# One fused attention and MLP kernel: another order of the prologue's steps, dummy products spread over it, and new tables behind it

## The chip, the cores and the metric

The kernel runs on one core of a Trainium2 chip. The metric is the device time of one execution in microseconds (us), as the median of several runs; less is better. Five engines work side by side, each through its own list of instructions in order: TensorE (PE, matrix products; its weight loads are shown as PEld), VectorE (DVE), ScalarE (ACT), GpSimd (POOL), and SyncE (SP), whose list issues nearly all transfers. An instruction starts when those before it on its engine have begun or ended and the semaphores that it waits for are there.

## What is computed

The reference, cut to what matters (8 batches, 8 heads, 576 tokens, head size 64; 4608 tokens of width 512, a hidden width of 2048):

```python
q_c, k_c, v_c = (a.reshape(B, H, nc, 64, D) for a in (q, k, v))
scores = np.matmul(q_c, k_c.transpose(0, 1, 2, 4, 3)) / np.sqrt(D)
attn = np.exp(scores - np.max(scores, axis=-1, keepdims=True))
attn = attn / (np.sum(attn, axis=-1, keepdims=True) + 1e-09)
x = np.matmul(attn, v_c).reshape(B, H, S, D).transpose(0, 2, 1, 3).reshape(B * S, H * D)
r = np.maximum(x @ w_in, 0.0)
out = (s * (r * r) + b) @ w_out
```

Each chunk of 64 tokens attends to itself alone; then every token goes through a squared-ReLU layer.

## The kernel before

**Numbers as pairs.** A float32 operand is split into a high part (names ending in h: `xh`, `wh`, `gh`) that TensorE takes in one pass and the remainder (`xl`, `wl`, `gl`). Each product is three: high by high, high by low, low by high.

**The prologue** (class `First`) does the first four token blocks of 128 with plain products while the weights are unpacked. There are 16 weight pairs, each a tile of 128 x 1024 in two halves .0 and .1, and pairs of w_in and w_out alternate: up 0 and 1 use pair 0, up 2 and 3 pair 1, down 0 and 1 pair 2, and so on. A pair goes through these steps: `load` (SP, into one of three `raw` buffers), `scale` and `tail` (ScalarE, L214 and L218), `shift` and `sign` (VectorE, L224 and L226), `add` (POOL, L232; it frees the raw buffer), `hi` (ScalarE, L236, makes `wh`), `lo` (VectorE, L240, makes `wl`), and `keep` (SP, L248, writes them to memory as `kept`). TensorE uses a pair in `up` and `more` (L904, x by w_in) or in `down` (L929, g by w_out); `left` is the first half of the columns of up 0. After an `up`, `relu` and `copy` (ScalarE, L909 and L913) and `rest` (VectorE, L917) make g and free its PSUM bank, of which there are two.

**Attention** of two token blocks takes the steps `load_qk`, `load_v`, `scores` (TensorE, L320), `peak` (VectorE, L325), `sub` (VectorE, L329), `exp` (ScalarE, L334), `sum` (VectorE, L338), `invert` (VectorE, L345 and L346), `scale` (L349: POOL for pair a, VectorE for pair b), `transposes` (TensorE, L356), `copies` (ScalarE, L361), `values` (TensorE, L383), `x_hi` (ScalarE, L406) and `x_lo` (VectorE, L410). Pairs .a and .b are the prologue's own; numbers (scores.0 and on) are the following block's, and a name like `2:scores.0` belongs to the block after that. From the fourth block on `turn` (VectorE, L367) and `swap` (SP, L376, eight small transfers) take the place of `transposes` and `copies`.

**Dummy products.** `keep_busy` (L179) multiplies a tile of ones by itself into a bank that nobody reads: steps `busy0` to `busy5` with 8, 6, 12, 2, 4 and 2 products. `scalars` (TensorE, L960) and `scalars_out` (VectorE, L963) bring the two scalars s and b into place.

**Behind the prologue** four blocks of eight token blocks use products of a Strassen-like kind (`1:p0` to `1:p57` in block 1; L839, L574, L623, 12 products each). The weights come back from `kept` through six buffers: `1:st6` is the transfer (L547) of the seventh. `combine`, `combined_hi`, `combined_lo` and `keep_combined` (L266, L272, L276, L279) form sums of weight quarters and write them to `kept` for these products, beside the products of block 1. `x_sums` (L505) forms sums of x.

**What sets the order.** Every step is a function under a name. The string `ORDER` lists 781 names, from the first load to the end of block 1, and the last line of the kernel calls them in that order, so the order of each engine's and each queue's instructions is that of the string. The blocks behind it follow a planner's rule. The string `SLOTS` gives each new SBUF tile its home: the number of one of 45 places of 4 KB per partition, in the order in which tiles are made. A tile that takes a place waits for those who still use what was there. The scheduler adds no order of its own (`tc.manual_schedule()`).

```python
order = ORDER.split()
for previous, block in zip([None] + blocks, blocks):
    order += [name for name in block.order(previous) if name not in order]
for name in order + blocks[-1].pre[-1]:
    ops[name]()
```

Of the kernel before, what the change touches and what calls it, by code (L numbers as in the profile page):

```python
# [31 lines left out]
scores.0 sign3.0 add2 relu0 rest1 peak.0 up3 copy0 rest0 lo1 load5 hi2 up2 tail3 lo2 keep2 more2 scale4 add3.0 sub.0
down0 load_v.0 tail4 shift4 hi3.0 sign4 relu2 down1 lo3.0 exp.0 add4 copy2 sum.0 scale5 rest2 tail5 more3 norm.0
add3.1 load6 up4 hi4 load7 hi3.1 more4 relu3 keep1 lo4 transposes.0 2:load_v.1 copies.0 shift5 down2 lo3.1 copy3 relu4
sign5 scale6 rest3 add5 up5 copy4 shift6 tail6 more5 load8 sign6 load_v.1 values.0 relu5 rest4 add6 scale7 down3 copy5
hi5 rest5 shift7 load9 hi6 up6 sign7 keep0 x_hi.0 lo5 x_out.0 up7 lo6 tail7 more6 scale8 x_lo.0 add7 more7 relu6
shift8 scores.1 tail8 load10 down4 relu7 sign8 scale9 peak.1 add8 copy7 down5 copy6 rest7 hi7 rest6 shift9 load11 hi8
lo7 keep3 tail9 up9 lo8 tail10 sign9 up8 scale10 sub.1 add9 more9 shift10 more8 relu9 down6 load12 copy9 sign10 keep7
exp.1 keep6 relu8 add10 sum.1 down7 load_v.2 copy8 rest9 hi9 norm.1 load13 tail11 up10 scale11 rest8 hi10 shift11
transposes.1 lo9 keep9 copies.1 up11 lo10 tail12 sign11 scale12 more10 more11 relu10 shift12 add11 sign12 values.1  # L40
down8 x_hi.1 load15 relu11 2:load_v.0 x_lo.1 add12 copy11 down9 hi11 keep8 rest11 copy10 x_out.1 rest10 load14 lo11
scale13 scores.2 keep5 hi12 shift13 up13 peak.2 tail13 keep4 sub.2 up12 load_qk.3 lo12 exp.2 more13 scale15 sum.2
more12 tail15 load_v.3 norm.2 down10 relu13 sign13 relu12 keep11 shift15 transposes.2 scale14 add13 down11 copy12
copy13 keep12 copies.2 rest13 shift14 hi13 values.2 rest12 tail14 sign14 up15 x_hi.2 lo13 add14 x_lo.2 up14 sign15
x_out.2 more14 hi14 more15 lo14 add15 scores.3 relu15 relu14 down12 peak.3 copy15 sub.3 stream hi15 down13 copy14 lo15
exp.3 rest14 rest15 2:load_qk.0 down14 sum.3 keep14 norm.3 last 1:combine0.7 keep13 transposes.3 copies.3 1:combine0.6
down15 values.3 1:combine1.0 steady 1:p0 x_hi.3 out0 x_lo.3 out1 1:p2 1:combine1.1 1:combined_hi0.7 x_out.3
1:keep_combined0.7.0 keep10 1:combine0.5 1:p1 keep15 1:combine1.2 1:combined_hi0.5 1:p4 1:combined_hi0.6
1:keep_combined0.5.0 1:combined_hi1.0 1:combine0.4 1:relu11.0 2:scores.0 1:combined_lo0.5 1:combined_hi0.4 1:p5
2:peak.0 1:combined_hi1.2 1:keep_combined0.4.0 1:combined_lo0.6 1:keep_combined1.2.0 1:combined_lo0.4 1:p6  # L50
1:keep_combined0.6.1 1:relu12.0 1:st6 1:st7 2:sub.0 2:load_qk.1 1:combined_hi1.1 1:combined_lo1.0 1:p3 2:exp.0
1:combined_lo0.7 1:combined_lo1.1 1:p7 1:relu21.0 2:sum.0 1:keep_combined1.1.1 2:norm.0 1:p8 2:turn.0 1:x_sums.0
2:swap.0.7 2:swap.0.4 1:p9 1:keep_combined0.6.0 2:swap.0.1 1:keep_combined0.5.1 1:x_sums.1 2:swap.0.3 1:p10 2:swap.0.0
1:xh2.1 2:swap.0.6 1:relu22.0 2:swap.0.5 1:combine1.3 1:keep_combined0.4.1 1:keep_combined0.7.1 1:p12 2:swap.0.2
1:xh3.1 1:xh4.0 1:keep_combined1.1.0 1:combine1.4 1:xh4.1 1:relu11.1 1:p11 1:st10 1:st11 1:combine1.5 1:xh2.0 1:gh0.0
1:p13 1:relu21.1 1:combined_lo1.2 1:st9 1:keep_combined1.0.1 1:combine1.6 2:values.0 1:st8 1:p14 2:x_out.0 1:xl4.0
1:combined_hi1.3 1:combined_hi1.4 1:keep_combined1.3.0 1:combined_lo1.3 1:keep_combined1.0.0 2:scores.1 1:xh3.0
1:xl2.1 1:xh6.0 1:relu12.1 1:xl2.0 1:p15 1:xl6.0 2:peak.1 1:st13 2:sub.1 1:p16 1:st12 2:load_qk.2 1:xl3.0 2:exp.1
1:xl3.1 1:keep_combined1.2.1 1:relu22.1 1:xl4.1 1:p17 2:sum.1 1:st15 1:keep_combined1.4.0 1:combined_lo1.4 1:keep0.2
1:xh6.1 2:norm.1 1:p18 1:combined_hi1.6 1:xl6.1 2:turn.1 1:p19 1:keep2.2 1:gl0.0 2:swap.1.4 2:swap.1.2 1:keep3.2  # L60
1:combine1.7 2:swap.1.6 1:st22 1:p21 2:swap.1.1 2:swap.1.7 1:form11.2 2:swap.1.3 1:st16 1:combined_lo1.6 1:st14
1:square11.2 1:p23 1:st18 1:keep_combined1.3.1 1:form21.2 1:p20 1:st17 1:keep0.3 2:swap.1.5 1:gh0.1 2:swap.1.0
1:keep_combined1.4.1 1:square21.2 1:p24 1:form22.2 1:less11.0 1:combined_hi1.5 1:gl0.1 1:p22 1:square22.2
1:keep_combined1.5.0 1:st19 1:less11.1 1:st20 1:keep3.3 2:values.1 1:st23 1:gh0.2 1:p25 2:x_out.1 1:gl0.2 1:form12.2
1:combined_lo1.5 1:less12.1 1:keep_combined1.5.1 2:scores.2 2:load_qk.3 1:keep2.3 1:less12.0 1:gh3.1 1:p26 1:st24
1:keep_combined1.6.1 2:peak.2 2:sub.2 1:p27 1:st28 1:form11.3 1:less11.2 1:square11.3 1:p28 1:gl3.1 1:st21 1:gh4.1
1:t2.0 1:combined_hi1.7 1:t2.1 1:p30 2:exp.2 1:keep_combined1.7.0 1:form21.3 1:st25 1:gh1.1 1:form22.3 1:p31 1:st26
1:combined_lo1.7 1:square22.3 2:sum.2 1:gh3.0 1:p32 2:norm.2 1:st27 1:keep_combined1.6.0 1:gh4.2 1:keep_combined1.7.1
1:less12.2 1:gh0.3 1:p29 1:gh1.0 column_sums 1:gl3.0 1:gh3.2 2:turn.2 1:p34 1:form12.3 1:gl0.3 2:swap.2.1 2:swap.2.7
1:combine0.2 1:st31 1:st29 2:xh0.0 1:p33 2:swap.2.5 1:gh2.0 1:less11.3 2:swap.2.6 1:gh1.2 2:swap.2.3 1:gl1.1  # L70
2:swap.2.2 1:square21.3 1:st30 1:gl3.2 1:st38 2:swap.2.4 1:less12.3 biases 1:p35 1:gh4.0 1:gh3.3 1:gl4.1 1:p36 1:st34
1:gh2.1 2:load_v.2 1:gl3.3 1:keep0.down 2:swap.2.0 1:gl2.0 1:p37 1:st32 1:t2.2 1:t2.3 1:gh2.2 1:gl1.2 1:p38 1:gh2.3
1:st33 1:keep3.down 1:gl2.1 1:gl1.0 2:values.2 1:st47 1:gl2.2 1:p39 2:x_out.2 1:gl2.3 2:xh0.1 1:combine0.0 1:gh5.0
finish 2:scores.3 1:st35 2:load_v.3 1:gl4.0 1:p40 2:peak.3 1:gh5.3 2:sub.3 1:p42 1:st36 1:less21.0 2:exp.3 1:gh5.2
2:sum.3 1:combined_hi0.0 1:less21.1 1:p41 1:st39 1:combined_hi0.2 1:combine0.1 2:xh1.0 1:gh1.3 1:p43 2:xl1.0 1:st41
1:combined_hi0.1 2:norm.3 1:gh6.0 1:keep2.down 2:turn.3 1:p44 1:gh6.1 1:combined_lo0.0 2:swap.3.3 1:gh4.3 1:st40
1:gh5.1 1:p46 1:gl4.2 1:st42 1:keep_combined0.0.1 2:xh1.1 2:swap.3.5 1:gl4.3 2:swap.3.0 1:combined_lo0.2 1:p47 1:st37
1:gl5.3 1:gl6.0 1:p48 1:st43 1:gl1.3 2:swap.3.2 1:keep_combined0.2.0 1:gl5.0 1:keep_combined0.1.0 1:p49 1:st46
1:less21.3 2:swap.3.7 2:swap.3.1 1:less21.2 2:swap.3.6 1:combine0.3 2:swap.3.4 1:gh6.2 1:p45 1:keep_combined0.0.0
1:gh6.3 1:st44 1:gl6.2 2:xh5.0 1:combined_hi0.3 1:p50 1:gl6.3 1:st45 1:gl6.1 1:combined_lo0.1 1:p51 2:xl5.0  # L80
1:keep_combined0.1.1 1:st49 1:gl5.2 1:gl5.1 2:values.3 1:st48 3:load_qk.0 1:end11 1:p52 2:x_out.3 3:load_v.0 1:end00
2:x_sums.1 2:xl0.1 1:p54 2:st1 store 1:p53 2:st0 2:x_sums.0 2:xh6.1 2:xh5.1 2:xl6.1 1:p55 2:st4 2:xh4.0 2:xh3.1
1:end10 1:scaled00 2:xl0.0 1:p56 1:scaled10 2:xl3.1 2:xh2.1 1:store10 2:xh3.0 1:store00 1:p57 2:xh2.0 2:st2 2:xl3.0
2:st3 2:xh6.0 1:keep_combined0.3.0 2:xh4.1 2:xl4.0 1:end01 2:xl2.0 2:xl6.0 1:scaled11 2:xl1.1 2:xl5.1 2:xl2.1
1:store11 2:xl4.1 1:combined_lo0.3 1:keep_combined0.3.1 1:keep_combined0.2.1 2:st5
"""


# [992 lines left out]
```

## Time and profile before

| | |
|---|---|
| time, median of 3 runs | 786.87 us (786.78 to 787.15) |
| the profiled execution | 787.23 us; span from its first to its last instruction 785.4 us |
| TensorE busy | 770.5 us (98%) |
| VectorE, ScalarE, POOL busy | 547.6, 486.1, 156.5 us |
| mean granted clock of TensorE | 0.993 of full speed |
| transfers | 206.42 MB, 263 GB/s on average |

The profile shows one execution. Spans of instructions are in us from the first instruction; "idle before <-" names what ended the time in which the engine stood still. A matmul of float32 operands is shown as two rows, so 14 dummy products are 28 rows. Matmuls overlap, so the spacing of their starts is their cost, not the length of one. The span and the 1.83 us around it make up the execution's own time.

### The profile page before, as it was taken

Reading aid. Unit: us, or ns where it says so; the run is one execution under the profiler, and the core shown is the slowest. Engines: PE = TensorE matmul, PEld = TensorE weight load, DVE = VectorE, ACT = ScalarE, POOL = GpSimd, SP = SyncE. Lnnn points to the kernel's source line nnn. Section 1 sums busy time; section 2 is a strip of 40 time slices with the busy share of each in tenths; the row PEclk is TensorE's granted clock in tenths of the full one; section 3 lists DMA queues with packets and bytes.
Section 4 is the critical chain, followed back from the end, with each engine's and each line's share of the span. In section 5 each row is a group of like instructions: output and inputs, shape, how many; then the busy total and the mean of one; then the engine's idle time right before and its main releaser. Section 6 shows DMA issues by size and latency. Waiting matters only on the chain.

```text
span 785.4 us, 13747 instructions
## 1 busy us (share of the span) xinstructions
PE 770.5 (98%) x5538; PEld 634.6 (81%) x5538; DVE 547.6 (70%) x569; ACT 486.1 (62%) x582; POOL 156.5 (20%) x74
## 2 busy tenths in 40 slices
...
GB/s 321 283 274 331 332 383 300 294 281 368 348 306 267 224 374 360 264 291 246 214 255 168 280 256 279 291 172 285 187 270 225 239 251 193 189 192 195 200 217 108
DMA packets 86818, 206.42 MB, mean 263 GB/s; under 512 B 8036, under 2 KB 37988, under 8 KB 86756
## 3 DMA queue, kind: packets, MB, share of 16 engines
...
q10 hardware_dynamic: 148, 0.13, 0.1%
...
## 4 chain that ended last, share of the span: by engine, by line
PE 94%; DVE 2%; ACT 2%; issue 1%; DMA 1%; DVEq 0%; SPq 0%; ACTq 0%
PE ps_o L623 26%; PE ps_o L574 25%; PE ps L623 11%; PE ps L574 10%; PE ps_h L904 4%; PE ps_o L929 4%; PE ps_o L839 4%; PE ps L839 2%; PE ps_a L383 2%; PE ps_a L317 2%; PE ps_o L638 1%; PE ps_h L179 1%; DVE wl L240 1%; PE ps_a L356 1%; DMA qk<-in_qkv_dram 1%
## 5 line engine op out<-in xcount | busy, mean ns | idle before, releaser
L623 PE MATMUL ps_o<-gh,st 128*128 128x512 f32 x608 | 190.7, 390 | 0.0
L602 DVE TENSOR_TENSOR gl<-q,gh 128x1024 fp32r<-128x1024 f32 x112 | 156.4, 1425 | 47.6 <-ACT gh L597 45.5
L574 PE MATMUL ps_o<-xh,st 128*128 128x512 f32 x560 | 180.9, 392 | 0.0
L623 PEld LDWEIGHTS ps_o<-gh,st 128*128 128x128 f32 x608 | 114.1, 188 | 24.0
L597 ACT CAST gh<-q 128x1024 fp32r<-128x1024 f32 x112 | 113.4, 1047 | 28.5 <-DVE q L610 28.2
L610 POOL TENSOR_TENSOR q<-q 128x1024 f32<-128x1024 f32 x24 | 66.6, 2782 | 323.3 <-PE ps_o L574 212.6
L574 PEld LDWEIGHTS ps_o<-xh,st 128*128 128x128 f32 x560 | 105.1, 188 | 23.6 <-DMA st<-kept 0.3
L623 PE MATMUL ps_o<-gl,st 128*128 128x512 f32 x304 | 118.3, 389 | 0.0
L574 PE MATMUL ps_o<-xl,st 128*128 128x512 f32 x280 | 109.1, 390 | 0.0
L455 DVE TENSOR_TENSOR q<-ps_o,tmp 128x1024 f32<-128x1024 f32 x28 | 34.3, 1224 | 77.7 <-PE ps_o L574 59.8
L623 PE MATMUL ps<-gh,st 128*128 128x512 f32 x256 | 81.4, 391 | 0.0
L574 PE MATMUL ps<-xh,st 128*128 128x512 f32 x224 | 73.5, 389 | 0.0
L580 ACT ACTIVATE q<-q 128x1024 f32<-128x1024 f32 x42 | 44.3, 1054 | 36.4 <-DVE q L455 36.4
L623 PEld LDWEIGHTS ps_o<-gl,st 128*128 128x128 f32 x304 | 57.1, 188 | 11.7
L574 PEld LDWEIGHTS ps_o<-xl,st 128*128 128x128 f32 x280 | 52.6, 188 | 10.3
L449 ACT COPY tmp<-ps_o 128x1024 f32<-128x1024 f32 x37 | 37.3, 1008 | 37.5 <-PE ps_o L574 22.7
L610 DVE TENSOR_TENSOR q<-q 128x1024 f32<-128x1024 f32 x40 | 50.4, 1269 | 13.0 <-ACT q L593 12.6
L505 POOL TENSOR_TENSOR xt<-xf 128x512 f32<-128x512 f32 x12 | 21.8, 1814 | 185.4 <-DMA st<-kept 168.3
L880 ACT ACTIVATE o<-o,bias,sb 128x512 f32<-128x512 f32 x28 | 21.1, 807 | 57.8 <-DVE o L455 57.8
L232 POOL TENSOR_TENSOR f<-f,raw 128x1024 int32<-128x1024 int32 (+1 forms) x18 | 41.8, 2322 | 73.9 <-DVE f L226 30.0
L623 PEld LDWEIGHTS ps<-gh,st 128*128 128x128 f32 x256 | 48.0, 188 | 10.1
L623 PE MATMUL ps<-gl,st 128*128 128x512 f32 x128 | 49.8, 389 | 0.0
...
## 6 DMA issues: line engine op xcount, KB each, us to landing
st<-kept SPq DMA_DIRECT2D x218, 512.0 KB, 4.4
qk<-in_qkv_dram SPq DMA_DIRECT2D x36, 512.0 KB, 5.9
raw<-in_w_dram SPq DMA_DIRECT2D x32, 512.0 KB, 7.0
kept<-wh SPq DMA_DIRECT2D x20, 512.0 KB, 5.9
...
out_dram<-o SPq DMA_DIRECT2D x17, 512.0 KB, 6.5
kept<-f SPq DMA_DIRECT2D x16, 512.0 KB, 6.3
...
```

What stands on the lines that cost most here:

```text
L232: nc.gpsimd.tensor_tensor(out=i, in0=i, in1=low.bitcast(I32), op=ALU.add)
L449: nc.scalar.copy(out=self.u[product], in_=self.bank_of(product))
L455: nc.vector.tensor_tensor(out=to, in0=self.ps[bank], in1=self.u[kept], op=ALU.add)
L574: nc.tensor.matmul(out=to[:, k], lhsT=a[:, cols], rhs=x[:, c, :], start=i in BEGINS and c == 0 and n == 0, stop=c == 1 and n == 2, skip_gr ...
L580: nc.scalar.activation(out=q, in_=q, func=AF.Relu)
L597: nc.scalar.copy(out=self.g[i, pp][0], in_=self.q[quarter, pp])
L602: nc.vector.tensor_tensor(out=lo, in0=self.q[quarter, pp], in1=hi.bitcast(F32), op=ALU.subtract)
L610: engine.tensor_tensor(out=self.q[to, pp], in0=self.q[x, pp], in1=self.q[y, pp], op=ALU.subtract)
L623: nc.tensor.matmul(out=self.to[i][:, d], lhsT=a[:, cols], rhs=x[:, k, :], start=i in BEGINS and pp == 0 and k == 0 and n == 0, stop=pp == ...
L839: nc.tensor.matmul(out=bank[:, k], lhsT=a, rhs=x[:, c, :], start=d == 0 and c == 0 and n == 0, stop=d == 1 and c == 1 and n == 2)
L904: nc.tensor.matmul(out=self.h[j][:, cols], lhsT=w[c][low], rhs=x[:, c, :], start=low + c + i == 0, stop=low == 1 and c == NHP - 1)
L929: nc.tensor.matmul(out=self.acc[d], lhsT=a, rhs=x, start=(j == 0 and i == 0), stop=(j == NJ - 1 and i == 2))
```

## The change

Two strings are replaced: `ORDER`, with the same 781 names in another order, and `SLOTS`. Nothing else differs: the number of dummies in each `busy` step, the functions and the planner stay. The first lines of `ORDER` and one line of each table:

```diff
@@ -24,85 +24,85 @@
 ORDER = """
-load_qk.a load0.0 load_qk.b load0.1 load_v.a scores.a load1 busy0 peak.a load2 tail0.0 busy1 scale0.0 sub.a scalars
-busy2 shift0.0 exp.a scalars_out sign0.0 busy3 load_v.b busy4 sum.a add0.0 scores.b invert.a hi0.0 peak.b scale.a
...
+load_qk.a busy0 load0.0 load_qk.b load0.1 load_v.a scores.a load1 scalars peak.a busy1 load3 tail0.0 scale0.0 sub.a
+scores.b shift0.0 exp.a sign0.0 load_v.b add0.0 sum.a busy2 tail0.1 scalars_out invert.a hi0.0 peak.b scale.a scale0.1
...
 SLOTS = """
...
-43 44 1 2 3 4 7 5 11 10 8 18 0 14 15 25 27 24 28 30 34 21 26 31 39 40 22 9 23 13 42 1 32 33 25 15 27 28 21 3 10 13 43
...
+43 44 1 2 3 4 7 5 11 10 0 8 16 14 15 22 21 31 32 25 41 20 23 33 37 38 24 42 29 44 9 18 15 22 11 16 20 13 29 30 34 31
...
```

What this does to the instructions is read at three places. In such a list a dummy row counts products, not the profile's rows.

TensorE at the start of the program, before the change. `qk` feeds scores.a and, in its second row, scores.b; `ident,p` are transposes.a and .b, `pT,v` values.a and .b, `ones` the dummies, `sb_row` the scalars, and `xh,wh` the first product of the layer:

```order
L320 MATMUL ps_o<-qk 64x64 x32
L179 MATMUL ps_h<-ones 128x128 x14
L960 MATMUL ps_h<-ident,sb_row 128x1 x2
L179 MATMUL ps_h<-ones 128x128 x18
L320 MATMUL ps_o<-qk 64x64 x32
L356 MATMUL ps_a<-ident,p 128x128 x8
L383 MATMUL ps_o<-pT,v 64x64 x32
L356 MATMUL ps_a<-ident,p 128x128 x8
L383 MATMUL ps_o<-pT,v 64x64 x32
L179 MATMUL ps_h<-ones 128x128 x2
L904 MATMUL ps_h<-xh,wh 128x256
```

The same place after the change:

```order
L179 MATMUL ps_h<-ones 128x128 x8
L320 MATMUL ps_o<-qk 64x64 x32
L960 MATMUL ps_h<-ident,sb_row 128x1 x2
L179 MATMUL ps_h<-ones 128x128 x6
L320 MATMUL ps_o<-qk 64x64 x32
L179 MATMUL ps_h<-ones 128x128 x12
L356 MATMUL ps_a<-ident,p 128x128 x8
L179 MATMUL ps_h<-ones 128x128 x2
L383 MATMUL ps_o<-pT,v 64x64 x32
L179 MATMUL ps_h<-ones 128x128 x4
L356 MATMUL ps_a<-ident,p 128x128 x8
L179 MATMUL ps_h<-ones 128x128 x2
```

Of the 32 dummies that stood between scores.a and scores.b six are left there; eight stand ahead of scores.a, and the others between the later attention steps.

VectorE in the same stretch, as a difference: from sub.a and shift0.0 (`f<-f`) by sign0.0 (`f<-raw,f`), sum.a (`z<-p`) and the copy of the scalars (`sb<-ps_h`) to invert.a (`z<-z`):

```order
 L329 TENSOR_TENSOR p<-ps_o,m 128x2x8x64
 L224 TENSOR_SCALAR f<-f 128x512
+L226 SCALAR_TENSOR_TENSOR f<-raw,f 128x512
+L338 TENSOR_REDUCE z<-p 128x16
 L963 COPY sb<-ps_h 128x2
-L226 SCALAR_TENSOR_TENSOR f<-raw,f 128x512
-L338 TENSOR_REDUCE z<-p 128x16
 L345 TENSOR_SCALAR z<-z 128x16
 L346 RECIPROCAL z<-z 128x16
```

The copy of the scalars has moved behind sign0.0 and sum.a.

SP beside the first streamed products of block 1, before the change: `kept<-wh` and `kept<-f` are keep_combined, `st<-kept_1_81 x2` are st6 and st7, `qk` the next block's load, `pT<-pB` swaps:

```order
L279 DMA kept_2_82<-wh 128x4x256 x2
L279 DMA kept_1_85<-wh 128x4x256
L279 DMA kept_3_83<-f 128x4x256
L547 DMA st<-kept_1_81 128x1024 x2
L294 DMA qk<-in_qkv_dram 128x1024 x2
L279 DMA kept_0_84<-f 128x4x256
L376 DMA pT<-pB 32x512 x2
```

The same place after the change:

```order
L294 DMA qk<-in_qkv_dram 128x1024 x2
L302 DMA v<-in_qkv_dram 128x512 x2
L279 DMA kept_3_83<-wh 128x4x256
L547 DMA st<-kept_1_81 128x1024
L376 DMA pT<-pB 32x512
L547 DMA st<-kept_1_81 128x1024
L376 DMA pT<-pB 32x512 x4
```

A swap, which waits for `turn`, now stands between st6 and st7.

## Rows read from the trace of the kernel before

**Rows 1.** The page, part 1: busy time and its share of the span.

```profile
PE 770.5 (98%) x5538; PEld 634.6 (81%) x5538; DVE 547.6 (70%) x569; ACT 486.1 (62%) x582; POOL 156.5 (20%) x74
```

**Rows 2.** What TensorE waited for: us in total, times, longest us.

```profile
PE ps_o L320 <- DMA qk<-in_qkv_dram: 4.3, 1, 4.3
PE ps_o L383 <- ACT pT L361: 3.8, 2, 3.1
PE ps_a L356 <- DVE p L349: 1.9, 1, 1.9
PE ps_o L929 <- DVE wl L240: 0.9, 1, 0.9
```

**Rows 3.** The chain of waits, 0 to 40 us: start us, us, what.

```profile
5.63 1.13 PE ps_o L320 x32
6.76 4.32 PE ps_h L179 x28
11.28 4.21 PE ps_h L179 x36
15.50 1.14 PE ps_o L320 x64
17.91 1.23 DVE p L329
22.51 1.22 DVE p L349
37.86 2.40 PE ps_h L904 x9
```

**Rows 4.** Stretches, `ps_h` alone: us, PE, PEld, DVE, ACT, clock, DMA share, GB/s.

```profile
8.00:8.50 0.50, 0.50 (x4) 0.50 (x4) 0.00 (x0) 0.00 (x0) 1.00 1.07 442
9.50:10.00 0.50, 0.50 (x7) 0.50 (x6) 0.00 (x0) 0.00 (x0) 1.00 0.95 377
```

**Rows 5.** Stretch, all work: us, PE, PEld, DVE, ACT, POOL, clock, DMA, GB/s.

```profile
23.00:32.65 9.65, 8.11 (x90) 7.52 (x91) 8.85 (x11) 7.51 (x12) 2.40 (x1) 0.50 0.96 352
```

**Rows 6.** Timeline of VectorE: start us, us, instruction [idle before].

```profile
11.32 0.16 DVE L963 COPY sb<-ps_h 128x2 f32<-128x2 f32 x1 [1.68 <-PE ps_h L960]
21.96 0.63 DVE L240 TENSOR_TENSOR wl<-f,wh 128x512 fp32r<-128x512 f32 x1
27.47 2.29 DVE L240 TENSOR_TENSOR wl<-f,wh 128x512 fp32r<-128x512 f32 x1 [0.80 <-ACT wh L236]
29.69 1.27 DVE L410 TENSOR_TENSOR xl<-ps_o,xh 128x512 fp32r<-128x512 f32 x2
```

**Rows 7.** Timeline of POOL.

```profile
14.00 1.90 POOL L349 TENSOR_TENSOR p<-p,z 128x1024 f32<-128x1024 f32 x1 [0.46 <-DVE z L346]
26.81 2.40 POOL L232 TENSOR_TENSOR f<-f,raw 128x1024 int32<-128x1024 int32 x1 [5.18 <-DVE f L226]
34.03 2.75 POOL L232 TENSOR_TENSOR f<-f,raw 128x1024 int32<-128x1024 int32 x1 [4.82 <-DVE f L226]
```

**Rows 8.** Transfers issued between 2.55 and 3.06: KB, us to landing.

```profile
qk<-in_qkv_dram SPq DMA_DIRECT2D x1, 512.0 KB, 7.0
```

**Rows 9.** Timeline of ScalarE.

```profile
28.54 0.59 ACT L406 CAST xh<-ps_o 128x512 fp32r<-128x512 f32 x1 [0.27 <-PE ps_o L383]
```

**Rows 10.** Stretches, all work, columns as in rows 5.

```profile
31.00:121.00 90.00, 89.00 (x817) 72.88 (x816) 78.92 (x89) 78.53 (x116) 36.77 (x15) 0.99 0.93 320
121.00:291.00 170.00, 170.00 (x1280) 139.35 (x1281) 154.60 (x202) 109.26 (x128) 2.78 (x2) 1.00 0.91 311
```

**Rows 11.** The chain of waits, 150 to 170 us.

```profile
156.98 8.16 PE ps_o L839 x36
```

**Rows 12.** Block 1: SP and VectorE timelines; transfers issued 119 to 300 us.

```profile
148.96 2.36 SPq L547 DMA_DIRECT2D st<-kept  x2
156.88 1.25 DVE L367 STREAM_TRANSPOSE pB<-p 128x1024 f32<-128x1024 f32 x1
st<-kept SPq DMA_DIRECT2D x53, 512.0 KB, 5.8
```

More of the change, by code (lines that the diff above doesn't have):

```diff
@@ L26 @@
 ORDER = """
-load_qk.a load0.0 load_qk.b load0.1 load_v.a scores.a load1 busy0 peak.a load2 tail0.0 busy1 scale0.0 sub.a scalars
-busy2 shift0.0 exp.a scalars_out sign0.0 busy3 load_v.b busy4 sum.a add0.0 scores.b invert.a hi0.0 peak.b scale.a
-scale0.1 tail0.1 sub.b shift0.1 exp.b transposes.a sign0.1 copies.a sum.b add0.1 values.a scale1 invert.b load3 tail1
-lo0.0 load_qk.0 scale.b x_hi.a load_qk.2 shift1 transposes.b x_lo.a copies.b values.b sign1 hi0.1 x_hi.b busy5 lo0.1
-add1 left x_lo.b scale3 up1 scale2 shift3 tail2 load4 more1 hi1 shift2 load_qk.1 sign3.1 up0 relu1 sign2 more0 copy1
@@ L32 @@
[L32 to L85, printed above, removed]
+load_qk.a busy0 load0.0 load_qk.b load0.1 load_v.a scores.a load1 scalars peak.a busy1 load3 tail0.0 scale0.0 sub.a
@@ new lines @@
+scores.b shift0.0 exp.a sign0.0 load_v.b add0.0 sum.a busy2 tail0.1 scalars_out invert.a hi0.0 peak.b scale.a scale0.1
+sub.b shift0.1 exp.b transposes.a sign0.1 busy3 copies.a sum.b add0.1 values.a scale1 invert.b load2 hi0.1 busy4
+scale.b load_v.1 x_hi.a shift1 load_qk.0 transposes.b tail1 x_lo.a busy5 copies.b sign1 values.b scale3 lo0.0 add1
+x_hi.b left x_lo.b scale2 up1 lo0.1 tail2 load4 hi1 shift2 more1 shift3 up0 relu1 sign2 more0 sign3.0 add2 copy1
+scores.0 relu0 rest1 up3 copy0 tail3 rest0 lo1 load5 up2 hi2 add3.0 load_v.0 peak.0 scale4 load_qk.2 more3 lo2 hi3.0
@@ new lines @@
+more2 tail4 sign3.1 down0 relu3 shift4 add3.1 sub.0 relu2 sign4 load6 down1 copy2 copy3 exp.0 lo3.0 add4 rest2 hi3.1
+rest3 tail5 up4 sum.0 scale5 lo3.1 load7 more4 hi4 norm.0 load_qk.1 up5 relu4 keep1 shift5 scale6 lo4 more5
+transposes.0 sign5 copies.0 down2 shift6 add5 relu5 sign6 tail6 values.0 copy4 scale7 load8 down3 copy5 shift7 add6
+hi5 rest4 x_out.0 rest5 sign7 tail7 up6 load9 x_hi.0 up7 load_v.2 lo5 hi6 add7 keep2 scale8 x_lo.0 more7 tail8 more6
+lo6 relu7 scores.1 load10 hi7 keep0 down4 shift8 relu6 sign8 copy6 peak.1 copy7 add8 scale9 down5 rest6 rest7 shift9
@@ new lines @@
+hi8 load11 lo7 up9 tail9 sign9 scale10 more9 lo8 add9 tail10 up8 sub.1 relu9 more8 shift10 down6 load12 hi9 sign10
+keep6 exp.1 copy9 add10 down7 relu8 rest9 sum.1 copy8 scale11 norm.1 load13 up10 hi10 keep3 rest8 tail12 keep8
+transposes.1 lo9 keep4 copies.1 up11 shift11 scale12 lo10 tail11 values.1 sign11 more11 x_hi.1 add11 more10 relu11
+x_lo.1 down8 copy11 load14 x_out.1 rest11 shift12 relu10 sign12 scores.2 scale13 add12 down9 hi11 peak.2 copy10 sub.2
+load15 lo11 up13 exp.2 keep10 hi12 rest10 keep11 sum.2 more13 tail13 up12 shift13 relu13 norm.2 scale14 more12 lo12
@@ new lines @@
+keep12 transposes.2 relu12 sign13 down10 copy13 load_qk.3 tail15 rest13 add13 keep5 shift14 copy12 scale15 keep9
+down11 copies.2 rest12 hi13 tail14 lo13 values.2 shift15 up15 x_hi.2 sign14 x_lo.2 add14 up14 sign15 x_out.2 more14
+hi14 more15 lo14 keep14 scores.3 add15 relu15 relu14 down12 peak.3 load_v.3 copy14 2:load_qk.0 sub.3 copy15 hi15
+stream rest14 down13 rest15 exp.3 lo15 sum.3 down14 norm.3 2:load_v.1 1:combine1.0 down15 keep13 last 1:combine0.5
+transposes.3 copies.3 steady 1:p0 1:combine0.4 out0 1:combined_hi1.0 1:x_sums.0 1:combined_hi0.5 values.3
@@ new lines @@
+1:combined_hi0.4 1:p2 x_hi.3 1:keep_combined0.4.0 1:combined_lo0.5 keep7 out1 1:combined_lo0.4 1:keep_combined0.5.1
+keep15 1:p1 1:combine0.6 1:keep_combined0.5.0 1:keep_combined1.0.0 x_lo.3 1:combined_hi0.6 2:load_qk.1 1:p3
+1:combine0.7 x_out.3 1:relu11.0 2:load_v.0 1:combined_lo1.0 2:scores.0 1:p4 2:peak.0 2:sub.0 1:combined_lo0.6 1:p6
+2:exp.0 1:xh3.0 2:sum.0 1:relu21.0 2:norm.0 1:p5 1:combined_hi0.7 1:combine1.1 1:keep_combined0.7.0 1:st6 1:p8
+2:turn.0 1:x_sums.1 2:swap.0.0 1:p9 1:st7 2:swap.0.2 1:xh2.1 2:swap.0.4 1:relu12.0 2:swap.0.7 1:combined_lo0.7 1:p7
@@ new lines @@
+2:swap.0.5 1:keep_combined0.6.0 1:combine1.2 2:swap.0.3 2:swap.0.1 2:swap.0.6 1:p10 1:combined_hi1.2
+1:keep_combined0.6.1 1:combine1.3 1:keep_combined0.4.1 1:combined_hi1.1 1:keep_combined1.0.1 1:combined_hi1.3 1:p11
+1:combined_lo1.1 1:relu22.0 1:combined_lo1.2 1:p12 1:combined_lo1.3 1:relu11.1 1:xl3.0 1:keep_combined1.3.1 1:st8
+1:combine1.4 1:keep_combined1.2.1 2:values.0 1:st9 1:combined_hi1.4 1:p13 2:x_out.0 1:combined_lo1.4 1:st13 1:relu21.1
+1:combine1.5 1:p14 1:st10 1:keep_combined1.4.1 1:xh3.1 1:keep_combined1.1.0 1:xh4.1 1:combine1.6 1:xh4.0 1:xh6.1
```

28 lines of the change are left out of this document (added), and 26 rows, old and new, of the table SLOTS.

## The prediction

> **What bounds the kernel now.** I read the page first: TensorE is busy for 770.5 us, 98% of the span [rows 1]. Such a kernel gets faster only where TensorE does no useful work, so the next view is what TensorE waited for: four, 10.9 us together: for the first qk, for pT (twice), for p, and once 0.9 us for wl, late in the prologue [rows 2]. Behind the prologue there is none: to the end the chain is TensorE at 8.16/36 = 0.2267 us a product [rows 11]; a lead that TensorE gains in the prologue comes off the end in full, unless a new wait takes it back.
>
> The chain of the first 40 us shows the loss [rows 3]. scores.a waits for the second qk tile and ends at 6.76 us. Then come 28 and 36 rows of dummies, 4.32 + 4.21 us (a dummy product is two rows), and only then scores.b, at 15.50. Everything of the second pair of token blocks (peak, sub, exp, sum, scale, transposes, values) hangs on scores.b, and the chain runs through it. Its qk had landed long before: the later tile was issued at 2.59 and took 7.0 us, so it was there at 9.6 [rows 8]. So the dummies are on the path, and where TensorE waits, after transposes.a and before transposes.b, there are none. In that stretch the granted clock goes to its lower level: 0.50 (1.2 of 2.4 GHz) from 23.00 to 32.65, with TensorE busy for 8.11 of these 9.65 us [rows 5], after waits of 3.1 and 1.9 us [rows 2]. VectorE has a loss of its own: its copy of the scalars waits 1.68 us for a TensorE step behind the first dummies, and sign0.0 stands behind it [rows 6].
>
> **The change part by part.** The same 781 steps are issued, so no work is added or removed; 34 dummy products stay 34. I replay the new order from these durations: half-size steps on ScalarE and VectorE 0.53 to 0.69, full ones 1.07 to 1.29, POOL's scale 1.90 and its full add 2.40 [rows 7], its half add 1.3 (an estimate: half of that and a little).
>
> *Start.* Eight dummies (16 rows) now come first. The clock column says 1.00 there, but dummies pass at four rows in half a us at 8.0 and seven at 9.5 [rows 4], so the early pace is half. At twice 4.21/36 us a row, 16 rows take 3.74 us: from the memset's end at 1.00 to about 4.75, past the landing of the first qk tile (4.35, the first wait of [rows 2]). Two halves of scores.a at the slow 1.13 us [rows 3] end at 7.0, 0.25 later than before. If the earlier activity raises the pace sooner, it is 6.2; I keep 7.0 and put the 0.8 into the range.
>
> *scores.b.* Six dummies (12 rows) end by 9.5, then scores.b ends at 10.6. VectorE: peak.a, sub.a to 9.55, shift0.0 and sign0.0 (no longer behind the scalars) to 10.5, sum.a 10.7 to 11.9 after exp.a, copy and invert to 12.55, peak.b to 13.8, sub.b to 15.1. Before, sub.b ended at 17.91 + 1.23 = 19.14: VectorE's path leads by 4.0. exp.b, sum.b, invert, then scale.b 17.9 to 19.15, against 23.73 [rows 3]: 4.6.
>
> *TensorE's gaps.* scale.a on POOL, 12.6 to 14.5 (1.90, [rows 7]); 24 dummy rows until 13.4, transposes.a 14.5 to 15.4; copies.a on ScalarE behind exp.b, 16.2 to 17.3; values.a to 17.85; eight dummy rows; transposes.b 19.2 to 20.1. ScalarE now does scale1, hi0.1, x_hi.a and tail1 ahead of copies.b, so copies.b ends at 22.3 and values.b at 22.85. TensorE's gaps are under 1.3 us each, with dummies in four of them, against 3.1 and 1.9; I take the higher level from here. scale3 stands before x_hi.b, which ends at 24.6 (before 28.54 + 0.59 = 29.13, [rows 9]). "left" is 12 products of 256 columns, 22.9 to 24.3. up1 then waits for x_lo.b, 25.35 (before 29.69 + 1.27 = 30.96, [rows 6]), and it and more1 end at 27.9; up0 and more0 29.3, scores.0 30.5. up3, which waits for relu1, copy1 and rest1 to free its bank, starts at 30.5. Before it started at 37.86 [rows 3]. **TensorE's lead is 7.3 us.** Of it 7.0 is scores.b's earlier place and the dummies off the path, the rest the clock and small waits, less 0.25 at the start. The 34 dummies cost nothing here but these 0.25, because each group ends before what comes next is ready.
>
> *The rest of the prologue.* VectorE's lead at x_lo.b is 5.6, less the half lo0.1 that now stands behind it (0.65): 4.95. To keep 7.3, VectorE has to give up 2.35 us of the time in which it idled between 31 and 121, 90.0 - 78.92 = 11.1 us. ScalarE has 11.5 us idle [rows 10], leads by 4.5 and has scale3 behind it already, 5.6: it needs 1.7. Nothing between 0 and 2.35 is excluded; I take the middle, 1.2 lost. Lead at the first streamed product: 6.1.
>
> *Block 1.* Here the tables move the streamed weights. Before, st6 and st7 were issued at 148.96, ahead of all swaps; now st7 stands behind swap.0.0, which waits for VectorE's turn.0. Before, turn.0 ended at 156.88 + 1.25 = 158.13, 24.5 us after the first streamed product, which began at 133.67 (the 156.98 of [rows 11], where p8 begins, less eight streamed products of 2.72 us, one attention step of 1.1 and two changes of shape of some 0.2) [rows 12]. Now VectorE has x_sums.0 before it but less of combine; added up it ends 24 us after. Issue of swap and stream 1.2, landing 5.8 [rows 12]: 31.0. p10 starts 29.8 after (ten streamed products and two attention steps) and first reads st7 half way, at 31.2. So it just fits. st11 takes the buffer that p15 frees in its first half, and p19 reads it 1.36 + 5.44 + 0.2 = 7.0 us later; the tightest such case before was 7.6. With 5.8, and single loads of 6 to 7, I charge 0.8 us for both: below, 0 (both fit), above 3 (a landing of 8 twice). Sum: 7.3 - 1.2 - 0.8 = 5.3. The profiled execution took 787.23, so 781.9; the median of the runs shown is 0.36 below it: **781.6 us**.
>
> A row and a rule that speak against it: wl on VectorE took 2.29 us at 27.47 beside an add on POOL, where half a tile takes 0.63 at 21.96; and POOL's add took 2.75 at 34.03 against 2.40 at 26.81, which I read as POOL held back by the VectorE instruction that had begun first [rows 6, 7]. The new order puts lo0.0, with both inputs in SBUF, right at the start of POOL's add1. The Trainium skill (SBUF — State Buffer, "Who interferes with whom") says that such an instruction and a GpSimd one that reads SBUF exclude each other for a whole instruction, and that the one issued first has the port. By it lo0.0, next on its own queue after sign1, should go first, as in the row of 34.03, and the sum stays; the other way round is priced in the first rival.
>
> **Rivals.** *VectorE and ScalarE set the pace* (chance 0.2): they were busy for 88% and 87% of 31 to 121, and VectorE for 91% of 121 to 291 [rows 10]. If POOL's add1 wins that port, up1's wl waits for lo0.0 until 25.9 and x_lo.b and up1 shift by 1.8; with all of the 2.35 lost too and 0.8 in block 1: 7.3 - 1.8 - 2.35 - 0.8 = 2.35 left, 784.5. *The dummies do not hold the clock* (0.07): a stretch like that of [rows 5] returns and half of its 8.11 busy us is lost, 4.05; 5.3 - 4.05 = 1.2, 785.6 us, no measurable change. *Slower* (0.13): the stream in block 1. Every us by which turn.0 is late beyond the fit above delays st7, p10 and what is queued behind p10 one for one. Faster turns into slower when 6.1 + 1.6 = 7.7 us are lost there, that is when turn.0 ends over 32 us after the first streamed product; 10 us lost give 790.8. For it: VectorE is 91% busy and the queue stands still behind one waiting swap. Against it: VectorE's list up to there is no longer than before. *The lead is larger* (0.1): the early pace saves 0.8 and nothing is lost later: 8.1, 778.8.
>
> **The numbers.** The forecast has 0.5, and its own range is 779.5 to 783.5. The 8-in-10 range goes from the larger lead, 778.5, through the two smaller gains to 786.8. A measurement of this kernel can tell about 0.2% (1.6 us) from no change. Faster by more than that: 0.5 + 0.1 + 0.18 of the first rival + 0.02 = 0.80; within it 0.05 of the clock rival and 0.02 of the first, 0.07; slower 0.13.
>
> **What would show it.** Right: scores.b at 9.5 instead of 15.5; no granted clock below 1.00 between 15 and 40; up3 at 30.5; the first streamed product near 127.6; TensorE's waits there and after under 2 us in all. Wrong: a TensorE wait on st of several us around p10 or p19, or on wl between 60 and 120.

## The result and the profile after

The changed kernel takes 777.70 us (median of 4 runs, 777.38 to 778.25); the kernel before took 786.83 us beside it (785.79 to 787.15). The ratio is 0.9887, with a 95% interval of 0.987 to 0.9904: faster by 1.1%. The prediction, 781.6 us, named the direction and the main mechanism, but the time lies 0.8 us below its range. The profiled execution took 777.77 us, its span is 776.0 us, 9.4 less than before.

The page's busy times (against [rows 1]) and what TensorE waited for (against [rows 2]; us in total, times, longest):

```profile
PE 767.9 (99%) x5538; PEld 632.6 (82%) x5538; DVE 544.1 (70%) x569; ACT 486.7 (63%) x582; POOL 158.5 (20%) x74
```

```profile
PE ps_h L179 <- DVE one_col L165: 1.1, 1, 1.1
PE ps_h L904 <- DVE g L917: 0.7, 2, 0.4
PE ps_o L383 <- ACT pT L361: 0.7, 2, 0.4
PE ps_a L356 <- POOL p L349: 0.6, 1, 0.6
PE ps_o L320 <- DMA qk<-in_qkv_dram: 0.5, 1, 0.5
PE ps_a L356 <- DVE p L349: 0.4, 1, 0.4
PE ps_h L904 <- DVE xl L410: 0.3, 1, 0.3
```

The long waits for the first qk, for pT and for p have shrunk to pieces of 0.6 us at most; the first line only says that the dummies themselves wait for their ones. The 0.9 us for wl near the end of the prologue is gone as well, and there is no wait on st.

The chain of waits, 0 to 40 us (start us, us, what), against [rows 3]:

```profile
1.05 3.79 PE ps_h L179 x16
4.84 1.96 PE ps_o L320 x64
...
13.26 0.92 DVE p L329
...
15.68 1.29 POOL f L232
...
17.37 6.66 DMA raw<-in_w_dram
...
25.15 1.16 ACT raw L218
...
28.98 0.70 DVE g L917
...
29.73 5.73 PE ps_h L904 x24
```

The last row is up3: 29.73 where it was 37.86, a lead of 8.1 us. What ends last ahead of it is new: load2 (the transfer of 6.66 us) had to wait for the raw buffer that add0.1 frees, and scale2, tail2, hi1, relu1 and rest1 follow it. The chain of waits from 122 to 138 us, where the first streamed products stand, shows what became of the lead:

```profile
122.87 0.87 PE ps_a L356 x8
123.74 2.73 PE ps L839 x12
126.48 1.09 PE ps_a L383 x64
127.57 2.95 PE ps_o L839 x12
```

p2, the last of these rows, began at 136.62 before: 9.05 us. The last products of the program (L638) began at 761.58 against 770.82: 9.2. So nothing of the lead was lost, and 0.9 us more was won on the way. The rows, two from the kernel before and one from the change:

```profile
136.62 2.72 PE ps_o L839 x12
770.82 10.89 PE ps_o L638 x48
```

```profile
761.58 10.89 PE ps_o L638 x48
```

Stretches (us, PE, PEld, DVE, ACT, POOL, clock, DMA share, GB/s), against [rows 5] and [rows 10]:

```profile
23.00:32.65 9.65, 8.95 (x106) 7.43 (x105) 7.71 (x11) 8.59 (x13) 5.10 (x3) 1.00 0.74 266
31.00:113.00 82.00, 81.63 (x722) 66.69 (x721) 74.25 (x84) 72.91 (x106) 35.23 (x14) 1.00 0.94 327
113.00:283.00 170.00, 170.00 (x1280) 139.69 (x1282) 153.98 (x202) 110.12 (x129) 6.93 (x5) 1.00 0.94 319
```

The granted clock stays at 1.00 (2.4 GHz), and VectorE is busy for 91% of the stretch from 31 to 113, against 88% of 31 to 121 before.

### The profile page after: what moved, and what is told of

The parts are those of the page before. It is cut to its first block, busy times and chain, and to the rows that moved or that the text cites. A ratio compares the mean times of both kernels' runs of the same rounds, so it can differ in the third digit from the quotient of the medians.

```text
span 776.0 us, 13758 instructions
## 1 busy us (share of the span) xinstructions
PE 767.9 (99%) x5538; PEld 632.6 (82%) x5538; DVE 544.1 (70%) x569; ACT 486.7 (63%) x582; POOL 158.5 (20%) x74
## 4 chain that ended last, share of the span: by engine, by line
PE 96%; DVE 1%; ACT 1%; DMA 1%; issue 0%; POOL 0%; DVEq 0%; SPq 0%; POOLq 0%; ACTq 0%
PE ps_o L623 27%; PE ps_o L574 25%; PE ps L623 11%; PE ps L574 10%; PE ps_h L904 5%; PE ps_o L929 5%; PE ps_o L839 4%; PE ps L839 2%; PE ps_a L383 2%; PE ps_a L317 2%; PE ps_o L638 1%; DMA raw<-in_w_dram 1%; PE ps_h L179 0%; PE ps_a L356 0%; PE ps_a L320 0%
## 5 line engine op out<-in xcount | busy, mean ns | idle before, releaser
L232 POOL TENSOR_TENSOR f<-f,raw 128x1024 int32<-128x1024 int32 (+1 forms) x18 | 44.3, 2461 | 65.5 <-DVE f L226 20.6
```

What stands on the lines that cost most here:

```text
L232: nc.gpsimd.tensor_tensor(out=i, in0=i, in1=low.bitcast(I32), op=ALU.add)
```

## The experiments

In their rows most line numbers are one lower than in the kernels above (L178 for L179). Positions of two steps tell the cases apart: up3, the end of the early prologue, and p2. They are from each kernel's profiled execution. Kernels with one list up to there differ too: up3 lay between 29.46 and 30.00 in the change and the four with a delay, and at 30.29 and 29.65 in b_list and b_list_lo. Each ratio is to runs of the kernel before beside it, whose medians differ by 0.4 us.

| kernel | time us | ratio to before (95%) | up3 | p2 | span |
|---|---|---|---|---|---|
| before | 786.83 | | 37.86 | 136.62 | 785.4 |
| the change | 777.70 | 0.9887 (0.987 to 0.9904) | 29.73 | 127.57 | 776.0 |
| b_list | 780.51 | 0.9913 (0.9894 to 0.9932) | 30.29 | 128.94 | 779.2 |
| a_late | 785.42 | 0.9975 (0.9965 to 0.9986) | 37.39 | 135.22 | 783.8 |
| a_none | 778.69 | 0.9893 (0.9876 to 0.991) | 30.39 | 128.20 | 776.8 |
| b_none | 780.22 | 0.9908 (0.9883 to 0.9933) | 32.21 | 130.99 | 779.7 |
| a_busy0 | 779.12 | 0.9897 (0.9882 to 0.9911) | 31.31 | 129.14 | 777.7 |
| a_dve | 777.70 | 0.9881 (0.9864 to 0.9898) | 29.62 | 127.35 | 775.9 |
| a_dve8 | 781.30 | 0.9924 (0.9907 to 0.9941) | 29.46 | 129.68 | 779.7 |
| a_turn | 778.45 | 0.989 (0.9875 to 0.9905) | 30.00 | 127.84 | 777.1 |
| a_turn6 | 784.27 | 0.9962 (0.9947 to 0.9977) | 29.64 | 127.45 | 782.0 |
| b_list_lo | 779.29 | 0.99 (0.9879 to 0.9922) | 29.65 | 127.44 | 776.1 |
| a_best | 778.45 | 0.9889 (0.9874 to 0.9904) | 29.06 | 127.84 | 776.5 |
| a_swap23 | 780.20 | 0.9909 (0.9893 to 0.9926) | 29.20 | 128.68 | 779.2 |

### TensorE's list alone, and everything but TensorE's list

b_list, the kernel before with the change's order on TensorE:

```diff
-load_qk.a load0.0 load_qk.b load0.1 load_v.a scores.a load1 busy0 peak.a load2 tail0.0 busy1 scale0.0 sub.a scalars
-busy2 shift0.0 exp.a scalars_out sign0.0 busy3 load_v.b busy4 sum.a add0.0 scores.b invert.a ...
+load_qk.a busy0 load0.0 load_qk.b load0.1 load_v.a scores.a scalars busy1 scores.b busy2 load1 peak.a load2 tail0.0 ...
+... transposes.a busy3 ... values.a busy4 ... transposes.b busy5 ... values.b ...
```

> The kernel before with TensorE's prologue list of the change alone (dummies in six places, scores.b ahead of most of them); all other steps and homes stand as before. Theory 1 (the gain is TensorE's list: scores.b no longer behind 32 dummies): scores.b starts by 10, up3 near 31.2 us, a lead of 6.7, and about 1 us of it lost behind the prologue: 781 us, from 779.5 to 782.5. Rival (the other engines' new order carries most of it): up3 after 34, 784 or more.

a_late, the reverse on the changed kernel:

```diff
-load_qk.a busy0 load0.0 ... scores.a load1 scalars peak.a busy1 load3 tail0.0 scale0.0 sub.a
-scores.b ... busy2 ... busy3 ... busy4 ... busy5 ... values.b
+load_qk.a load0.0 ... scores.a busy0 busy1 scalars busy2 busy3 busy4 scores.b load1 peak.a load3 ...
+... values.b busy5
```

> The change with TensorE's prologue list of before: all dummies but the last two between scores.a and scores.b, none later; everything else as after. Theory 1: scores.b at about 15.5 again, a wait of 3 us of TensorE behind transposes.a, up3 near 37, 785.5 us (784 to 787). Rival (the other engines' order carries it): 782 or less.

Theory 1 holds. TensorE's list of the first attention steps alone leads by 7.6 us at up3 (8.2 in b_list_lo, below, with the same list there) and 7.7 at p2. Everything else of the change leads by 0.5 at up3 and 1.4 at p2. Added, 9.1, the lead of the full change; that it fits so closely is partly luck, given the 0.6 between two runs of one list. In a_late the stretch at 0.50 of [rows 5] returned (granted clock 0.50 from 24 to 28), in b_list it did not.

b_list ends with 6.2 of its 7.7 us. What TensorE waited for there, two of eight rows, and two rows of its chain of waits, 184 to 206 us, behind the first:

```profile
PE ps_a L382 <- DMA pT<-pB: 1.2, 1, 1.2
...
PE ps_o L928 <- DVE wl L239: 0.9, 1, 0.9
```

```profile
191.69 7.95 DMA pT<-pB
...
199.68 1.26 PE ps_a L382 x63
```

One of the last two swaps took 7.95 us to land (the median of the 32 between 119 and 300 us is 4.8), and 2:values.1 stood behind it. The 0.9 us for wl is the same as before the change, although TensorE comes 7.7 us earlier: so it is not a matter of how far VectorE is behind as a whole.

### The wait for wl

VectorE's and POOL's timelines where it arises, of the kernel before, then of b_list:

```profile
117.45 3.45 DVE L240 TENSOR_TENSOR wl<-f,wh 128x1024 fp32r<-128x1024 f32 x1
117.40 2.40 POOL L232 TENSOR_TENSOR f<-f,raw 128x1024 int32<-128x1024 int32 x1 [1.16 <-DVE f L226]
```

```profile
107.59 2.07 DVE L225 SCALAR_TENSOR_TENSOR f<-raw,f 128x1024 uint32<-128x1024 uint32 x1
109.76 3.47 DVE L239 TENSOR_TENSOR wl<-f,wh 128x1024 fp32r<-128x1024 f32 x1
```

```profile
109.74 2.42 POOL L231 TENSOR_TENSOR f<-f,raw 128x1024 int32<-128x1024 int32 x1 [1.17 <-DVE f L225]
```

The last sign releases POOL's last add, which begins 0.02 us ahead of lo14 (0.05 in the kernel before), and lo14 takes 3.47 us where other whole wl take 1.22. In b_list_lo two steps move, so that lo14 runs before that sign (three entries of SLOTS follow the new order of tiles):

```diff
-sign15 x_out.2 more14 hi14 more15 lo14 add15
+more14 hi14 lo14 sign15 x_out.2 more15 add15
```

> The kernel before with TensorE's prologue list of the change, and near the end of the prologue's weights hi14 ahead of x_out.2 on ScalarE and lo14 ahead of sign15 on VectorE, so that lo14 no longer starts beside POOL's last add (there it takes 3.45 us where others take 1.22). Theory 1 (the 0.9 us for wl is this one collision): no wait on wl near 113 us, p2 at 128.05 instead of 128.94, and 0.9 us less than with the list alone. Rival (ScalarE and VectorE as a whole are that late there): the wait stays or stands at the next wl, p2 at 128.9.

Rows of VectorE in b_list_lo, and two of its chain of waits, 120 to 130 us:

```profile
109.07 1.23 DVE L239 TENSOR_TENSOR wl<-f,wh 128x1024 fp32r<-128x1024 f32 x1 [2.00 <-ACT wh L235]
110.21 1.22 DVE L225 SCALAR_TENSOR_TENSOR f<-raw,f 128x1024 uint32<-128x1024 uint32 x1
```

```profile
124.49 2.95 PE ps L838 x12
127.44 2.72 PE ps_o L838 x12
```

lo14 takes 1.23 us and the wait on wl is gone, as theory 1 said; p2 comes 1.5 us earlier, 0.9 of it from this and 0.6 because the wait for g at up3 was 0.4 in this execution and 1.0 in the other. So the list on TensorE and this one small move give the profiled execution that the whole new tables give, 776.1 against 776.0. Its median is higher by 1.6 us, with runs between 777.9 and 780.74; the late swap of b_list was not in the profiled one, and whether it is in the others no trace shows.

The changed kernel still has this pair side by side, in the same order of steps, but there lo14 begins 0.04 us ahead of the add, and it is the add that is held up, to 3.47 us:

```profile
110.46 1.23 DVE L240 TENSOR_TENSOR wl<-f,wh 128x1024 fp32r<-128x1024 f32 x1
110.50 3.47 POOL L232 TENSOR_TENSOR f<-f,raw 128x1024 int32<-128x1024 int32 x1 [1.17 <-DVE f L226]
```

What decides is under 0.1 us: lo14 also waits for hi14 on ScalarE, which ended 0.08 us after that sign in the kernel before and ends together with it in the change. All ten traces of the change and of kernels made from it have lo14 first by 0.03 to 0.05 us and at 1.22 or 1.23; the kernel before, b_list and b_none have the add first and lo14 at 3.45 to 3.47. The leads say the same: from up3 to p2 the change and six of the kernels made from it gain 0.9 to 1.0 us, b_list and b_none 0.1 at most, and b_list_lo 1.0.

A second place in the change is lo0.0, which begins ahead of POOL's add1:

```profile
21.51 0.68 DVE L240 TENSOR_TENSOR wl<-f,wh 128x512 fp32r<-128x512 f32 x1
```

```profile
21.73 2.76 POOL L232 TENSOR_TENSOR f<-f,raw 128x1024 int32<-128x1024 int32 x1 [4.76 <-DMA raw<-in_w_dram]
```

Here POOL is the one that is held up (2.76 against 2.43 to 2.45 for seven of its 14 whole adds). The Trainium skill (SBUF — State Buffer, "Who interferes with whom") says that a VectorE instruction with both inputs in SBUF and a GpSimd one that reads SBUF exclude each other, and that the one issued first keeps the port; these places agree with it.

### What the dummies are worth

Three kernels drop dummy products, whose results nobody reads: a_none and a_busy0 from the change, b_none from the kernel before.

```diff
-    for n, times in enumerate((8, 6, 12, 2, 4, 2)):
+    for n, times in enumerate((0, 0, 0, 0, 0, 0)):
```

(a_busy0: 8, 0, 0, 0, 0, 0.)

> The change without any dummy product. Theory 1 (the dummies cost 0.25 us at the start, and their work is to hold the clock): scores.a starts at 4.35, a stretch at a granted clock of 0.50 between 12 and 35 returns, and up3 comes 1 to 4 us later than in the change: 779 to 782 us. Rival (the dummies do nothing for the clock here): up3 at 29.5, 777.5 us, no stretch at 0.50.

> The kernel before without any dummy product. Theory 1 (taking them off the path is worth some 6 us, the clock that is lost without them some 2 to 4): scores.b starts by 10, a longer stretch at 0.50 than before's 9.65 us, 783 us (781 to 785.5). Rival (in the order of before the dummies were worth their place): 787 or more.

> The change with the first eight dummies alone, none in the later gaps. Theory 1 (the early start raises the pace, and the later dummies keep it): scores.a as in the change, but transposes.a or what follows passes at half pace or at a granted clock of 0.50 again, and the time is that of the run without any dummy or above, 778.3 to 780.5. Rival (the later dummies do nothing): 777.7.

Without any dummy the change loses 1.0 us in the median and 0.8 in the span, a little less than theory 1 had; the kernel before gains some 7 (ratio 0.9908; its four runs lie between 778.18 and 781.5, and the profiled one, the slowest, has a lead of 5.6 at p2), more than either theory had. With the first eight alone the change loses 1.4 in the median and 1.7 in the span. So most of the change's gain is to be had by deleting the dummies from the old order; the new places of the 34 are worth about 1 us. A row of TensorE's timeline of a_none, and then its stretches and those of a_busy0:

```profile
14.23 1.97 PE L355 MATMUL ps_a<-ident,p 128*128 128x128 f32 x8 [3.08 <-POOL p L348]
```

```profile
8.00:16.00 8.00, 4.04 (x72) 3.46 (x72) 7.63 (x13) 4.33 (x6) 3.53 (x3) 1.00 1.01 387
16.00:24.00 8.00, 6.37 (x148) 5.74 (x148) 6.58 (x10) 7.70 (x13) 2.36 (x2) 1.00 0.97 325
```

```profile
8.00:16.00 8.00, 3.84 (x72) 3.07 (x72) 7.66 (x12) 4.31 (x7) 4.03 (x3) 0.55 1.02 391
16.00:24.00 8.00, 6.82 (x141) 6.19 (x141) 6.60 (x11) 7.71 (x13) 2.35 (x2) 0.50 1.01 352
```

In a_busy0 theory 1 is seen as expected: eight dummies raise the pace (scores.a passes in 1.48 us), TensorE then waits, and the granted clock falls to 0.50 (1.2 GHz). In a_none the expected stretch at 0.50 did not come, and yet transposes.a takes 1.97 us, as in a_busy0, where it takes 1.09 in the change: half pace under a granted clock of 1.00, up to values.b at 21.56. The time lost is small in both, since TensorE waits there for VectorE and ScalarE anyway.

### How much reserve VectorE has

a_dve and a_dve8 add 2.4 and 4.8 us to VectorE in the change, behind norm.0; a_turn and a_turn6 add 2.4 and 7.4 us ahead of turn.0 (two, four and six of these sums; a_dve's edit):

```diff
+    def delay():
+        for _ in range(2):
+            nc.vector.tensor_reduce(out=spare, in_=ident.unsqueeze(1).to_broadcast([P, 8, P]), op=ALU.add, axis=AX.X)
...
-norm.0 load_qk.1
+norm.0 delay load_qk.1
```

> The change with 2.4 us of additional work on VectorE (two sums over a constant tile, read by nobody) right behind norm.0, at about 43 us. Theory 1 (VectorE's idle time between the prologue and the stream, 8.1 of 92.7 us in the change, is a reserve that takes what is asked of it): TensorE gets no wait over 0.3 us and the time stays, 777.7 us. Rival 1 (the prediction's term: half of what VectorE has to give up is lost): 1.2 us more, 778.9. Rival 2 (VectorE, busy 91% there, sets the pace): 2.4 us more, 780.1, with waits on wl or g.

> As the run with 2.4 us more on VectorE behind norm.0, but with 4.8 us. VectorE idles some 6.6 us between 43 us and the stream in the change. Theory 1 (that idle time is the reserve, and most of it can be used before anything is late): at most 1.2 us are lost, 777.7 to 778.9. Rival (2.4 us was all the reserve there is): 2.4 us are lost, 780.1, with waits on wl or g.

> The change with the same 2.4 us on VectorE right ahead of turn.0 in block 1, so that swap.0.0, and st7 behind it on SP, are issued 2.4 us later. Theory 1 (st7 has a reserve of 1.35 us in the change: issued at 148.02, landing 5.6 later, first read half way through p10 at 154.96): a wait on st of 1.0 us in p10 and about 778.7 us. Rival 1 (it just fitted, as the prediction put it): a wait of 2 to 2.4, 780. Rival 2 (the transfer has more room than that): no wait, 777.7.

> As the run with 2.4 us more on VectorE ahead of turn.0, but with 7.3 us: turn.0 ends 30.9 us after the first streamed product. Theory 1 (the prediction's slower case: beyond a fit of 1.4 to 2.4 us every us is lost one for one): 5 to 6 us lost, 783 to 784. Rival (VectorE is asked for other things there that are late first, as ScalarE's combined_hi was, and they catch up): less than 3 us lost, 780.5 or less.

The first 2.4 us cost nothing: same time, p2 at 127.35, no new wait. Of 4.8, TensorE waits 2.4 us, in one piece between 40 and 60 us:

```profile
PE ps_o L929 <- DVE wl L240: 2.4, 1, 2.4
```

So at that place the reserve is some 2.4 us, and what goes beyond it is lost. My theory of a larger reserve fell: VectorE still had idle time, but later than the wl that came due. The whole run loses 3.6 us, more than the rival's 2.4: p2 is 2.1 later, and 1.5 more go by 320 us, where TensorE waits 0.9 for st, for which it never waits in the change.

The delay ahead of turn.0 costs 0.75 us for 2.4, little more than executions differ by, and near the size that theory 1 had; but not by its way: in a_turn TensorE never waited for st. What it and its weight loads waited for in a_turn6, SP's timeline, its chain of waits there, and a stretch of that (columns as above):

```profile
PE ps_o L839 <- ACT q L844: 4.0, 1, 4.0
PEld ps_o L839 <- DMA st<-kept: 0.4, 1, 0.4
```

```profile
154.60 0.60 SPq L376 DMA_DIRECT2D pT<-pB  x1
155.30 0.53 SPq L547 DMA_DIRECT2D st<-kept  x1
```

```profile
157.50 7.37 PE ps_o L839 x24
```

```profile
158.50:161.50 3.00, 3.00 (x9) 2.17 (x8) 2.79 (x8) 1.58 (x3) 0.00 (x0) 0.50 0.93 280
```

VectorE's x_sums came late, ScalarE's cast of them (L523) stood ahead of q (L844), which frees TensorE's bank: 4.0 us. The next 24 products take 7.37 us where 24 take 5.44: behind the wait the granted clock is 0.50 (1.2 GHz) from 158.5 to 161.5, and a weight load waits 0.4 for st7, issued at 155.30. Little of these 1.9 us is a loss of its own, because the product behind the 24 needs the bank that the next q frees: that q ends at 164.37, and the product starts at 164.70. In a_turn 0.5 of the loss is a wait for this next q, too; on ScalarE it stands behind a cast (L272) that waits for VectorE's combine. Counted from p2, the product behind it starts 0.7 us later than in the change in a_turn and 5.9 in a_turn6: a reserve of 1.5 to 1.7, and beyond it one for one. In the median a_turn6 loses 6.6, a little over the 5 to 6 expected. st7's landing is not fixed: 5.6 us in the change, 4.2 in a_turn.

### Two attempts at a faster version

a_best drops two of the first eight dummies and lets relu1 and copy1 pass tail2; a_swap23 has pair 2 take the buffer and the place of pair 3 (seven entries of SLOTS follow the new order of tiles):

```diff
-enumerate((8, 6, 12, 2, 4, 2))
-tail2 load4 hi1 shift2 more1 shift3 up0 relu1 sign2 more0 sign3.0 add2 copy1
+enumerate((6, 6, 12, 2, 4, 2))
+load4 hi1 shift2 more1 shift3 up0 relu1 copy1 tail2 sign2 more0 sign3.0 add2
```

> The change with six dummies ahead of scores.a in place of eight, and on ScalarE relu1 and copy1 ahead of tail2 (sign2 behind it on VectorE). Theory 1 (these two stand on the path to up3): scores.a starts at 4.35, up3 at 29.0 instead of 29.73, and 777.0 us. Rival (the pace of scores.a falls without the two dummies, or VectorE's list sets up3): 777.7 or more.

```diff
-load1 ... load3 ... load2 ... scale3 ... x_hi.b left x_lo.b scale2 up1 lo0.1 tail2 ... copy0 tail3 ... hi2
+load1 ... load2 ... load3 ... scale2 ... x_hi.b tail2 left x_lo.b up1 lo0.1 ... copy0 ... hi2 scale3 tail3 shift3 sign3.0
```

> The change with load2, scale2 and tail2 ahead of pair 3's steps: load2 takes the raw buffer that load3 had, scale3 and tail3 stand behind hi2. Theory 1 (up3 waits at the end of a chain through load2's landing at 24.0 us): scale2 starts without a wait, relu1 at 26.5 instead of 27.14, up3 at 29.1 instead of 29.73, 777.2 us. Rival (pair 3 is late then): a wait on wh or wl of pair 3 near up4, and 777.7 or more.

Both bring up3 forward as expected, to 29.06 and 29.20, and both lose it at once, as the rivals had it. In a_best tail2 now stands ahead of relu0, and up2 waits 0.7 us for rest0's bank; p2 is 0.3 later. In a_swap23 TensorE waits 0.8 for a wl between 34 and 40 and 0.9 for g later; p2 is 1.1 later, and 1.3 more go near 295 us, where the first of three streamed products begins late and each takes 0.25 to 0.30 us more (the first two, from the chains of waits of a_swap23, then of the change):

```profile
295.81 3.02 PE ps_o L573 x12
298.83 2.97 PE ps L573 x12
```

```profile
294.35 2.72 PE ps_o L574 x12
297.07 2.72 PE ps L574 x12
```

In a_swap23 the first weight load of these products waits 0.5 us for xl from VectorE, and the profile names nothing for the other two; in a_dve8 0.9 us near the same place are waits on st. What delays these in some versions stays open. No version tried beats the change.

## Why the prediction was wrong in size

**The main mechanism was right.** scores.b's first half starts at 8.81 (predicted 9.5), the granted clock never leaves 1.00 between 15 and 40, and b_list shows that TensorE's list carries 7.6 us. Deleting the dummies shows the same thing from the other side.

**The lead at up3** was put at 7.3 and is 8.1. The replay came out late by small amounts: scores.a ends at 6.80 instead of 7.0, sub.b begins at 13.26 and ends at 14.5 instead of 15.1, "left" begins at 21.79 instead of 22.9. TensorE is through scores.0 at 29.35, 1.15 earlier than predicted, and 0.4 of it goes to the chain through load2's landing, which the replay did not have.

**"The rest of the prologue"** is the step that failed: it took 1.2 us away as the middle between 0 and 2.35 for idle time that VectorE would have to give up. VectorE gave up all of it (it idles 7.8 us of 31 to 113, 11.1 of 31 to 121 before) and had 2.4 us in hand (a_dve), though hardly more (a_dve8). The same step overlooked a gain: the 0.9 us for wl stood in [rows 2], and I never asked what ends that wait and whether the new order keeps it. Its cause is one collision with POOL (b_list_lo). The new tables have the same pair, but lo14 begins 0.04 us ahead there; nothing in the prediction's working leads to that, so this part of the gain was luck. From up3 to p2 the lead grows from 8.13 to 9.05 instead of falling by 1.2: 2.1 of the 4.1 us by which the sum was off; 0.8 come from the lead, 0.8 from the next step, 0.4 from the end.

**"Block 1"** charged 0.8 for st7 and st11. There is no wait on st in the change: 0. The place was rightly chosen as a tight one: turn.0 ended 23.6 us after the first streamed product (24 predicted), and 7.4 us more there cost 6.0 of the span, one for one beyond some 1.5, the slope that the slower rival had. But its way is ScalarE's q; for the transfer a weight load waited 0.4.

Sum, predicted and measured: 7.3 - 1.2 - 0.8 = 5.3; 8.1 + 0.9 + 0 + 0.2 (between p2 and the last products) + 0.2 (behind them) = 9.4.

**The rivals.** That VectorE and ScalarE set the pace is wrong for this order and, for VectorE, right 2.4 us further on; lo0.0 went ahead of POOL's add1. That the dummies don't hold the clock is wrong as to the clock (a_busy0), and its price was too high: half of the busy time at 0.50 was put at 4 us, and 1.4 are lost; TensorE waited there for the other engines in any case (2.9 us for p and 1.5 for pT in a_busy0). The larger lead was the true case; it had 0.1 at 778.8, and its 8.1 was the lead that was measured at up3, without the 0.9; it got there by the early pace alone, where several small terms of the replay did it.
